# The first unit of a fused attention and feed-forward kernel on natural key and value tiles, with its band masks added by matmul

## The chip, the cores and the metric

The kernel runs on one core of a Trainium2 chip. The metric is the device time of one execution in microseconds (us); lower is better. Six executions of the kernel before took 213.77 to 217.03 us, with a median of 214.46. A profile of one execution shows, for each engine, what ran when: PE (TensorE, the matmuls) with its weight loads (PEld), DVE (VectorE), ACT (ScalarE), POOL (GpSimd) and SP (SyncE, which here only issues DMA transfers).

## The reference

Inputs are q, k and v of shape (4 batches, 8 heads, 768 positions, 64), and two weight matrices, w_in (512 x 2048) and w_out (2048 x 512), all float32. Each position attends to the positions closer than 16 and to 24 block summaries; a feed-forward layer follows.

```python
block, window = (32, 16)
k_sum = k.reshape(B, H, nb, block, D).max(axis=3)
v_sum = v.reshape(B, H, nb, block, D).mean(axis=3)
scores_l = scale * q @ k^T                       # kept where |i - j| < 16
scores_s = scale * q @ k_sum^T + log(block)      # 24 columns
a = softmax(concat(scores_l masked, scores_s))
x = a @ concat(v, v_sum)                         # (4*768) x 512
h = x @ w_in;  g = h * sigmoid(1.702 * h);  out = g @ w_out
```

## The kernel before

**Units.** The 3072 tokens are worked in eight units of 384: unit u is half u%2 of batch u//2. A unit needs the attention of its half (four pairs of heads p = 0 to 3, a pair fills the 128 partitions), gives the transposed result xT (four tiles of 128 x 384), and then 64 matmuls `ph` with w_in (`ff_in`), each four followed by a sigmoid-GELU on ACT into `gT`. For units 0 and 1, `ff_out` multiplies `gT` by w_out (`po`). For the later batches the second matrix product is done as seven products instead of eight on groups of tiles: three groups a, b, c (class `Pair`), with products p1 to p7 written a1, b1 and so on, on sums formed on DVE; their accumulators are named px, pw and py. While PE does one unit's feed-forward, the attention of the next unit is put between its matmuls.

**Order.** Every engine's instructions are kept in the order in which the program text records them (class `_Ordered`), so a waiting instruction holds up all behind it on its engine. The text of lines 817 to 957 is the order of the first unit, written out by hand; `plan0` and `plan1` (lines 961 to 964) place attention steps between the `ff_out` matmuls of units 0 and 1; `todo`, `first` and `second` place others after a given `ff_in` group `nt`; `order` and `meet` (lines 1026 to 1030) give the sequence of the seven-product matmuls and the attention steps of the next batch after each of them ("s"/"S" scores with exponential and mask of a pair, "v"/"V" the value multiply of two pairs with its normalisation, "x"/"X" the transposition of the result, small letters for the first half of the batch).

**Score tiles.** A tile of 64 queries meets 128 key columns of `kx`: its own 64 keys, 32 neighbours of either side as far as needed, and for most units the 24 block sums. `score_tiles` does 12 matmuls per pair into one two-bank tile (`psb`, two buffers), ACT takes the exponential (128 x 768, `a_sb`), DVE multiplies by the 0/1 mask `mk` (in the first unit `mk0`), and PE multiplies with the rows of `vw`, which hold the values in the same arrangement (65th column of ones for the denominator). Values lie in `vw` twice: even tiles e=0 and odd tiles e=1 (`v_odd` copies even to odd, then row copies and block-sum copies on SP's queue, `halo_odd`, `halo_even`, `sum_dmas`, overwrite the neighbour and block-sum rows).

**The first unit.** k and q come on SP's queue, are cast, and transposed by matmul (`k_turn`, `q_turn`); `k_own` copies the transposed keys into `kx`, `k_max` reduces block maxima, `k_blocks` copies them into `ksz`, `k_sides` copies the 32 neighbour columns. Values come through POOL's queue (`load_v0`, tile `vb`); `v_own`, `v_even`, `v_before`, `v_after` copy them into `vw`. The block part is apart: `b_turn`, `b_exp`, `v_sum`, `v_copy` and `av_blocks`. `s_turn`, `s_exp`, `s_mask`, `av_near`, `v_norm` and `x_turn` take a pair through attention, and `ff_first` does the first two `ph` groups as the four xT tiles appear. w_in is loaded in four pieces of 512 columns on POOL's queue (`load_w_in`), the first piece early, one in the midst, two at the end, followed by the second half of q and four pieces of w_out.

**Batch 1** is loaded during unit 0 and its values are doubled on POOL after `load_qc(1)` (line 1016); PE transposes its keys in unit 1 (`tk` at nt 2, 4, 6, 8). **Batches 2 and 3** have `v_odd(n)` on POOL at the start of unit 2b (line 1063).

Of the kernel before, what the change touches and what calls it, by code (L numbers as in the profile page):

```python
# [13 lines left out]
ALU = mybir.AluOpType  # L14
# [21 lines left out]
def kernel(  # L36
# [66 lines left out]
    def load_v0(h0, h1):  # L103
        if h0 == 0:
            early["v"] = stage.tile([128, H, NJ, D], BF16, name="vb", tag="vf")
        pool.dma_start(out=early["v"][:, h0:h1].rearrange("p h j d -> p (h j) d"),
                       in_=v[0, h0:h1].rearrange("h s d -> (h s) d")
                       .rearrange("(a p) d -> p a d", p=128))
# [23 lines left out]
    def v_odd(b):  # L132
        for p in range(NP):
            r = rows_of(b % 2, p)
            pool.tensor_copy(out=r[:, :, 1], in_=r[:, :, 0])
# [30 lines left out]
    mk0 = consts.tile([128, 2, QT], BF16, name="mk0")  # L166
    dve.memset(mk0, 1.0)

    def masks0():
        reach = window - 1  # L170
        for e, own, side in ((0, 0, 96), (1, QT, 0)):
            sel(mk0[:, e, :], reach - own, -1, 1)
            sel(mk0[:, e, :], reach + own, 1, -1)
            pool.memset(mk0[side:side + 32, e, :], 1.0)
        sel(mk0[96:128, 0, :], reach - 32, -1, 1)
        sel(mk0[0:32, 1, :], reach - QT, 1, -1)
# [51 lines left out]
    def clear0(eng):  # L228

        for p in range(NP):  # L230
            eng.memset(kx[p][0][:, 0, 96:128], 0.0)
            k4 = kx[p][0].rearrange("p (j e) c -> p j e c", e=2)
            eng.memset(k4[:, JH:NJ, 0, 88:96], 0.0)
            eng.memset(k4[:, JH:NJ, 1, 24:32], 0.0)
            eng.memset(kx[p][0][:, NQ - 1, 48:64], 0.0)
        w5 = vw[0].rearrange("p (j e) h c -> p j e h c", e=2)
        eng.memset(w5[:, :, :, :, D:VC], 1.0)
        eng.memset(w5[64:96, JH:NJ, 0, :, D:VC], float(block))
        eng.memset(w5[0:32, JH:NJ, 1, :, D:VC], float(block))
        eng.memset(vw[0][96:128, 0], 0.0)  # L240
        eng.memset(ksz, 0.0)
        eng.memset(vs4, 0.0)
        v6 = vs4.rearrange("p (a g) c -> p a g c", g=4)
        for g in range(4):
            eng.memset(v6[g * 32:g * 32 + nb, :, g, D:D + 1], float(block))

    def load_w_in(c):
        wi = moe_w_in.rearrange("(ko ki) n -> ki ko n", ki=128)
        pool.dma_start(out=w_in_sb[:, :, c * 512:(c + 1) * 512],
                       in_=wi[:, :, c * 512:(c + 1) * 512])  # L250
# [46 lines left out]
    def raw_v(p):  # L297
        return early["v"][:, 2 * p:2 * p + 2].rearrange("p h j d -> p j h d")
# [20 lines left out]

    def idle(n):  # L320

        bank = st.get("idle")
        if bank is None:
            bank = next((t for t in two if any(t is r for r in read)), None)
        if bank is None:
            return
        for i in range(n):
            pe.matmul(out=bank[:, 0:128], lhsT=warm[:, 0:128], rhs=warm[:, 0:128],
                      start=True, stop=True)


    two, read = [], []

    def opened(t):
        two.append(t)
        del two[:-2]
# [79 lines left out]

    def k_own(p, eng):

        copy(eng, at(flat_kx(p, 0), 0, [[768, 2], [256, JH], [192, 2], [1, 64]]),
             at(st["K", p], 0, [[512, 2], [128, JH], [64, 2], [1, 64]]))  # L420

    def k_max(p):
        st["m", p] = ks0[p]
        dve.tensor_reduce(out=ks0[p].rearrange("p (j e n) -> p j e n", e=2, n=2),
                          in_=at(flat_kx(p, 0), 0, [[256, NJ], [192, 2], [block, 2], [1, block]]),
                          axis=AX.X, op=ALU.max)

    def k_blocks(p, eng):

        eng.tensor_copy(out=ksz[0:64, p, 0:nb], in_=st["m", p][0:64])  # L430
        eng.tensor_copy(out=ksz[64:128, p, 32:32 + nb], in_=st["m", p][64:128])

    def k_sides(p, eng):

        flat = flat_kx(p, 0)
        eng.tensor_copy(out=at(flat, 64, [[256, JH], [96, 2], [1, 32]]),
                        in_=at(flat, 192, [[256, JH], [-160, 2], [1, 32]]))
        eng.tensor_copy(out=at(flat, 256 + 96, [[256, JH], [-224, 2], [1, 32]]),
                        in_=at(flat, 256 - 32, [[256, JH], [32, 2], [1, 32]]))
# [10 lines left out]
    def q_copy(p, eng, half=0):  # L450

        if half == 0:
            copy(eng, qT[p][0][:, 0:HALF], st["Q", p][:, 0:HALF])
            if p == NP - 1:
                st["idle"] = st["Q", p]
# [4 lines left out]
    def s_turn(p):  # L460

        big = st["S", p] = psb.tile([128, 1024], F32, name="ps_s", tag="big")
        opened(big)
        score_tiles(big, p, 0, 0)
# [9 lines left out]
    def s_exp(p):  # L474
        a = a_sb[p] = attp.tile([128, 2, TH, QT], BF16, name="a_sb", tag="a_sb")
        act.activation(out=a.rearrange("p h t c -> p h (t c)"),
                       in_=st["S", p].rearrange("p (h c) -> p h c", h=2)[:, :, 0:HALF],
                       func=ACT.Exp, scale=scale)
        read.append(st["S", p])

    def s_mask(p, eng):
        a = a_sb[p].rearrange("p h (j e) c -> p (h j) (e c)", e=2)
        eng.tensor_mul(a, a, mk0.rearrange("p e c -> p (e c)").unsqueeze(1)
                       .to_broadcast([128, 2 * JH, 2 * QT]))
# [13 lines left out]
    def v_own(p, eng):  # L498

        copy(eng, rows_of(0, p)[:, 0:JH, 1], raw_v(p)[:, 0:JH])  # L500

    def v_even(p, eng):
        copy(eng, rows_of(0, p)[0:96, 0:JH, 0], raw_v(p)[0:96, 0:JH])

    def v_before(p, eng):

        copy(eng, rows_of(0, p)[96:128, 1:JH, 0], raw_v(p)[96:128, 0:JH - 1])

    def v_after(p, eng):
        copy(eng, rows_of(0, p)[0:32, 0:JH, 1], raw_v(p)[0:32, 1:JH + 1])  # L510

    def v_sum(p):
# [4 lines left out]
        for j in range(NJ):  # L517
            o = 20 - 4 * j
            pe.matmul(out=st["VT"][r, p * 128:p * 128 + 128], lhsT=E[:, o:o + 64],
                      rhs=early["v"][:, 2 * p:2 * p + 2, j],  # L520
# [12 lines left out]
    def av_near(p):  # L533

        if p == 0:
            st["idle"] = None
        st["V", p] = pmm.tile([128, 512], F32, name="ps_av", tag="mm")
        for hh in range(2):
            for j in range(JH):
                for e in range(2):  # L540
                    t = 2 * j + e
                    pe.matmul(out=pv_of(p)[e * 64:e * 64 + 64, hh, j, 0:D + 1],
                              lhsT=a_sb[p][:, hh, t, :],
                              rhs=vw[0][:, t, 2 * p + hh, 0:D + 1],
                              start=(hh == 0 and j == 0), stop=False, skip_group_check=True)
# [15 lines left out]
    def x_turn(p):  # L561
        src = x_sb.pop(p)
        st["X", p] = psb.tile([128, 2048], F16, name="ps_x", tag="big")
        opened(st["X", p])
# [266 lines left out]
    k_turn(1)  # L831
    k_own(0, act)
    cast_k(dve, 2, 0)
    cast_k(dve, 2, 1)
    k_sides(0, pool)
    load_v0(0, 2)
# [5 lines left out]
    k_blocks(0, dve)  # L842
    cast_k(act, 3, 0)
    k_sides(1, pool)
    k_own(2, act)
    cast_k(act, 3, 1)
    k_max(1)
    cast_q(pool, 1, 0)
    cast_q(act, 0, 0)
    k_sides(2, pool)  # L850
    k_turn(3)
    k_own(3, act)
    k_blocks(1, dve)
# [3 lines left out]
    cast_q(pool, 3, 0)  # L857
    load_w_in(0)
    k_max(2)
    cast_q(dve, 2, 0)  # L860
    k_blocks(2, pool)
    q_turn(2)
    k_max(3)
    q_copy(1, act)
    s_turn(0)
    k_sides(3, dve)
    dve.tensor_copy(out=identx, in_=ident)
    q_turn(3)
    q_copy(2, act)
    s_turn(1)  # L870
    k_blocks(3, pool)
    b_turn(0)
    b_turn(2)
    s_exp(0)
    b_turn(1)
    q_copy(3, dve)
    s_mask(0, dve)
    v_own(0, pool)
    v_even(0, pool)
    v_before(0, dve)  # L880
    v_after(0, dve)
    s_exp(1)
    v_sum(0)
    s_turn(2)
    b_exp(0)
    v_copy(0, act)
    v_own(1, pool)
    v_even(1, pool)
    b_turn(3)
    s_mask(1, dve)  # L890
    v_before(1, dve)
    v_after(1, dve)
    v_sum(1)
    s_turn(3)
    s_exp(2)
    v_copy(1, act)
    av_near(0)
    av_blocks(0, 0, D + 1)
    v_own(2, pool)
    v_even(2, pool)  # L900
    s_mask(2, dve)
    b_exp(1)
    v_norm(0)
    v_before(2, dve)
    v_after(2, dve)
    v_sum(2)
    s_exp(3)
    av_near(1)
    av_blocks(1, 0, D + 1)
    v_own(3, pool)  # L910
    v_even(3, act)
    v_copy(2, dve)
    v_norm(1)
    x_turn(0)
    v_sum(3)
    v_before(3, dve)
    v_after(3, dve)
    s_mask(3, dve)
    load_w_in(1)
    copy(act, xT[0][0], st["X", 0][:, 0:HALF])  # L920
    av_near(2)
    av_blocks(2, 0, D + 1)
    v_copy(3, act)
    x_turn(1)
    v_norm(2)
# [3 lines left out]
    copy(act, xT[0][1], st["X", 1][:, 0:HALF])  # L929
# [9 lines left out]
    load_w_in(2)  # L939
    load_w_in(3)  # L940
# [4 lines left out]
    for p in range(NP):  # L945
        pool.tensor_copy(out=rows_of(0, p)[:, JH:NJ, 0], in_=raw_v(p)[:, JH:NJ])
        dve.tensor_copy(out=rows_of(0, p)[:, JH:NJ, 1], in_=raw_v(p)[:, JH:NJ])
# [44 lines left out]
    for u in range(2):  # L992
# [4 lines left out]
        else:  # L997
            todo = {2: [lambda: tk(0, 1)], 4: [lambda: tk(1, 1)], 6: [lambda: tk(2, 1)],
                    8: [lambda: tk(3, 1), lambda: load_kc(2), lambda: load_vc(2)],
                    14: [lambda: halo_odd(w51, 0), lambda: vsum(1, range(NJ))],  # L1000
# [12 lines left out]
        if u == 0:  # L1013
            beside(1, -1)
            load_qc(1)
            v_odd(1)
# [5 lines left out]
        for i, (ms, part) in enumerate(order):  # L1022
# [3 lines left out]
    order = ["a7", "a6", "a2", "a5", "b1", "a3", "b7", "a4", "b6", "b2", "b5",  # L1026
             "c1", "b3", "c7", "c6", "c2", "c5", "b4", "c3", "c4"]
    meet = {"a7": ["s0", "s1"], "b1": ["v0"], "b7": ["x0", "s2", "s3"], "b2": ["v1"],
            "c1": ["x1", "S0", "S1"], "c6": ["V0"], "c5": ["X0", "S2", "S3"], "c3": ["V1"],
# [14 lines left out]
    for b in range(1, B):  # L1044
# [17 lines left out]
        if more:  # L1062
            v_odd(n)
# [65 lines left out]
```

## Time and profile before

| | us |
|---|---|
| median of six runs | 214.46 (213.77 to 217.03) |
| the profiled execution | 215.11 |
| its span in the profile | 213.4 |
| PE busy | 200.5 (94%) |
| DVE busy | 135.9 (64%) |
| ACT busy | 124.1 (58%) |
| POOL busy | 97.9 (46%) |
| start of the dense `ph` matmuls of unit 0 | 26.11 |

Span is from the first to the last event of the profiled execution. PE's busy time includes modelled ends of pipelined matmuls. All operations are recorded through one helper, so their line is that helper's (L28), and they have to be told apart by tiles: `out<-in` names the tile written and those read. An arrow after the idle time before an instruction names what released it. Engine names with a q (SPq, POOLq) are the issuing side of DMA transfers.

### The profile page before, as it was taken

Reading aid. Unit: us, or ns where it says so; the run is one execution under the profiler, and the core shown is the slowest. Engines: PE = TensorE matmul, PEld = TensorE weight load, DVE = VectorE, ACT = ScalarE, POOL = GpSimd, SP = SyncE. Lnnn points to the kernel's source line nnn. Section 1 sums busy time; section 2 is a strip of 40 time slices with the busy share of each in tenths; the row PEclk is TensorE's granted clock in tenths of the full one; section 3 lists DMA queues with packets and bytes.
Section 4 is the critical chain, followed back from the end, with each engine's and each line's share of the span. In section 5 each row is a group of like instructions: output and inputs, shape, how many; then the busy total and the mean of one; then the engine's idle time right before and its main releaser. Section 6 shows DMA issues by size and latency. Waiting matters only on the chain.

```text
span 213.4 us, 5415 instructions
## 1 busy us (share of the span) xinstructions
PE 200.5 (94%) x2138; PEld 135.4 (63%) x2138; DVE 135.9 (64%) x377; ACT 124.1 (58%) x238; POOL 97.9 (46%) x192
## 2 busy tenths in 40 slices
PE   7767699999999899999999999999999999999994
PEld 3335465555655466656778876566788866668883
DVE  5789866562994477969978760896666820357332
ACT  2658478354667459767823477587544667772120
POOL 5799988869899999108999200000000000000000
PEclk9969999999999999999999999999999999999999
DMA  5996999999999999979999948870084150000223
GB/s 150 304 136 102 164 276 208 208 166 175 212 99 161 185 184 176 124 143 209 175 152 179 202 149 148 194 146 14 0 95 124 45 187 0 0 0 28 74 74 123
DMA packets 97832, 29.31 MB, mean 137 GB/s; under 512 B 84384, under 2 KB 95328, under 8 KB 97808
## 3 DMA queue, kind: packets, MB, share of 16 engines
q0 software_dynamic: 66960, 12.85, 72.4%
q1 hardware_dynamic: 30848, 16.13, 31.4%
q8 instruction: 16, 0.26, 0.5%
q14 instruction: 8, 0.07, 0.1%
HBM read 27.26 MB, written 6.29 MB: 157 GB/s over the span
## 4 chain that ended last, share of the span: by engine, by line
PE 61%; DMA 18%; POOL 9%; DVE 3%; ACT 3%; SPq 2%; issue 2%
PE ph L28 29%; PE px L28 14%; DMA w_out_sb<-in_moe_w_out_dram 9%; PE pw L28 7%; POOL vw L28 5%; DMA vw<-in_v_dram 3%; DMA vw<-vs 3%; PE py L28 3%; PE ps_av L28 3%; SPq L28 2%; PE po L28 2%; PE ps_s L28 2%; DMA kf<-in_k_dram 2%; DVE ks L28 2%; ACT a_sb L28 1%
## 5 line engine op out<-in xcount | busy, mean ns | idle before, releaser
L28 PE MATMUL ph<-xT,w_in_sb 128*128 128x384 f16 x512 | 85.9, 326 | 1.1 <-DVE xT L28 1.1
L28 ACT ACTIVATE gT<-ph 128x384 f16<-128x384 f32 x128 | 60.9, 490 | 27.1 <-PE ph L28 26.9
L28 PEld LDWEIGHTS <-w_in_sb 128*128 128x128 f16 x512 | 49.4, 98 | 33.1 <-issue 1.3
L28 PEld LDWEIGHTS <-gT 128*128 128x128 f16 x384 | 36.1, 98 | 12.2
L28 ACT ACTIVATE a_sb<-ps_s 128x768 bf16<-128x768 f32 x32 | 24.5, 806 | 14.4 <-PE ps_s L28 14.4
L28 POOL DMA_DIRECT2D kb<-in_k_dram x24 | 19.8, 852 | 13.7 <-DMA kx<-kb 10.7
L28 DVE TENSOR_TENSOR a_sb<-a_sb,mk 128x768 bf16<-128x768 bf16 x32 | 18.2, 571 | 10.2 <-ACT a_sb L28 8.8
L28 PE MATMUL po<-w_out_sb,gT 128*128 128x512 f16 x96 | 23.1, 380 | 0.0
L28 PEld LDWEIGHTS <-ss 128*128 128x128 f16 x216 | 20.4, 98 | 3.9 <-issue 1.3
L28 ACT ACTIVATE t<-px 128x256 f32<-128x256 f32 x21 | 8.1, 383 | 23.6 <-PE px L28 22.4
L28 POOL DMA_DIRECT2D qb<-in_q_dram x24 | 19.8, 868 | 1.4 <-DMA vw<-in_v_dram 1.3
L28 PE MATMUL px<-ta,ss 128*128 128x256 f16 x144 | 18.7, 273 | 0.9 <-ACT t L28 0.9
L28 DVE TENSOR_TENSOR ss<-gT 128x512 f16<-128x512 f16 (+3 forms) x21 | 8.0, 380 | 16.7 <-ACT gT L28 16.7
L28 PE MATMUL pw<-tb,gT 128*128 128x256 f16 x144 | 18.6, 273 | 0.0
L28 DVE TENSOR_REDUCE ks<-kx 128x24 bf16<-128x768 bf16 x12 | 11.4, 949 | 9.3 <-DMA kx<-kb 9.2
L28 DVE TENSOR_TENSOR x<-ps_av,rc 128x384 f16<-128x384 f32 x28 | 15.6, 558 | 1.0
L28 POOL DMA_DIRECT2D vw<-in_v_dram x18 | 15.9, 936 | 0.3 <-issue 0.3
L28 ACT ACT_TABLE_LOAD x10 | 12.8, 1283 | 1.0 <-PEq L1113 0.8
L28 DVE TENSOR_TENSOR osb<-pw,t 128x256 f32<-128x256 f32 x18 | 7.6, 421 | 7.1 <-ACT t L28 3.6
L28 PEld LDWEIGHTS <-a_sb 128*64 128x64 bf16 x384 | 7.9, 111 | 5.7 <-issue 2.4
L28 PE MATMUL ps_av<-vw,a_sb 128*64 128x65 bf16 x384 | 9.8, 197 | 1.4 <-DMA vw<-vs 0.8
L28 DVE RECIPROCAL rc<-ps_av 128x6 f32<-128x6 f32 x32 | 6.1, 189 | 6.9 <-PE ps_av L28 6.3
(94 smaller groups left out, 231.7 us busy)
## 6 DMA issues: line engine op xcount, KB each, us to landing
out_dram<-osb SPq DMA_DIRECT2D x18, 256.0 KB, 4.9
kb<-in_k_dram POOLq DMA_DIRECT2D x24, 96.0 KB, 6.3
vw<-in_v_dram POOLq DMA_DIRECT2D x18, 128.0 KB, 6.2
qb<-in_q_dram POOLq DMA_DIRECT2D x24, 96.0 KB, 6.4
w_in_sb<-in_moe_w_in_dram POOLq DMA_DIRECT2D x4, 512.0 KB, 7.7
w_out_sb<-in_moe_w_out_dram POOLq DMA_DIRECT2D x4, 512.0 KB, 17.0
kf<-in_k_dram SPq DMA_DIRECT2D x8, 192.0 KB, 4.1
out_dram<-osb SPq DMA_DIRECT2D x12, 128.0 KB, 1.7
```

The costliest lines, as they stand in the source:

```text
L28: r = f(*a, **kw)
```

## The change

In the first unit, keys stay in natural tiles of 128 (`own_keys`, in the second key buffer), and values are used straight from `vb`, which gets a column of ones. A pair's scores are 128 queries by 128 keys for each of three tiles, a piece of 16 queries that reach the tile before and a piece of 32 that reach the tile after, packed in 512 columns per head. A mask of 0 and -30000 (`mk0`) is written into the same accumulator first, by a matmul with the identity, so the multiplication after the exponential is gone; the exponential covers 128 x 1024. The copies `k_sides`, `v_own`, `v_even`, `v_before`, `v_after` and `s_mask` go; `k_tiles` later copies the key tiles that the second half needs. The hand-written order of the first unit is rewritten: the second query copy and three of the four `v_copy` are on DVE, one `k_blocks` on ACT, two query casts on DVE; w_in comes in pieces of 256, 256, 512, 512 and 512 columns, all issued before the second half of q. `v_odd` runs on DVE, for batch 1 at nt 13 of unit 1, for batches 2 and 3 at nt 6 of unit 2b. `order` and `meet` are changed.

```diff
     def load_v0(h0, h1):
         if h0 == 0:
-            early["v"] = stage.tile([128, H, NJ, D], BF16, name="vb", tag="vf")
+            early["v"] = stage.tile([128, H, NJ, VC], BF16, name="vb", tag="vf")
+            dve.memset(early["v"][..., D:VC], 1.0)
...
     def v_odd(b):
-            pool.tensor_copy(out=r[:, :, 1], in_=r[:, :, 0])
+            dve.tensor_copy(out=r[:, :, 1], in_=r[:, :, 0])
...
-    mk0 = consts.tile([128, 2, QT], BF16, name="mk0")
+    mk0 = consts.tile([128, 512], BF16, name="mk0")
+    BEFORE, AFTER, SIDE = HALF, HALF + 2 * window, 2 * window
     def masks0():
+        def out(ap, base, pattern, cp):
+            pool.affine_select(out=ap, in_=ap, compare_op=ALU.is_ge, fill=-30000.0,
+                               base=base, pattern=pattern, channel_multiplier=cp)
...
+    def own_keys(p):
+        return flat_kx(p, 1)[:, 0:S]
     def k_own(p, eng):
-        copy(eng, at(flat_kx(p, 0), 0, [[768, 2], [256, JH], [192, 2], [1, 64]]),
-             at(st["K", p], 0, [[512, 2], [128, JH], [64, 2], [1, 64]]))
+        copy(eng, own_keys(p).rearrange("p (e c) -> p e c", e=2),
+             at(st["K", p], 0, [[512, 2], [1, HALF]]))
...
     def s_turn(p):
-        score_tiles(big, p, 0, 0)
+        for h in range(2):
+            pe.matmul(out=big[:, h * 512:(h + 1) * 512], lhsT=ident, rhs=mk0, start=True,
+                      stop=False, skip_group_check=True)
+        def part(col, kj, q0, n):
+            for h in range(2):
+                r = slice(h * 64, h * 64 + 64)
+                pe.matmul(out=big[:, h * 512 + col:h * 512 + col + n],
+                          lhsT=own_keys(p)[r, kj * 128:(kj + 1) * 128],
+                          rhs=qT[p][0][r, q0:q0 + n], start=False, stop=True, skip_group_check=True)
+        for j in range(JH):
+            part(j * 128, j, j * 128, 128)
+            part(AFTER + j * SIDE, j + 1, j * 128 + 128 - SIDE, SIDE)
+            if j:
+                part(BEFORE + (j - 1) * window, j - 1, j * 128, window)
...
     def av_near(p):
+        def part(hh, j, q0, col, n, vj, first=False):
+            pe.matmul(out=pv_of(p)[q0:q0 + n, hh, j, 0:D + 1], lhsT=a_sb[p][:, hh, col:col + n],
+                      rhs=early["v"][:, 2 * p + hh, vj, 0:D + 1], start=first, stop=False,
+                      skip_group_check=True)
...
+    load_w_in(0, 256)
...
+    load_w_in(256, 512)
...
+    load_w_in(512, 1024)
...
+    load_w_in(1024, 1536)
+    load_w_in(1536, 2048)
...
+                    13: [lambda: v_odd(1)],
                     14: [lambda: halo_odd(w51, 0), lambda: vsum(1, range(NJ))],
...
-            v_odd(1)
             busy(6)
...
-    order = ["a7", "a6", "a2", "a5", "b1", "a3", "b7", "a4", "b6", "b2", "b5",
+    order = ["a7", "a2", "a6", "b1", "a5", "b7", "a3", "a4", "b6", "b2", "b5",
              "c1", "b3", "c7", "c6", "c2", "c5", "b4", "c3", "c4"]
-    meet = {"a7": ["s0", "s1"], "b1": ["v0"], "b7": ["x0", "s2", "s3"], "b2": ["v1"],
-            "c1": ["x1", "S0", "S1"], "c6": ["V0"], "c5": ["X0", "S2", "S3"], "c3": ["V1"],
+    meet = {"a7": ["s0", "s1"], "a5": ["v0"], "a4": ["x0", "s2", "s3"], "b5": ["v1"],
+            "b3": ["x1", "S0", "S1"], "c6": ["V0"], "c5": ["X0", "S2", "S3"], "c3": ["V1"],
             "c4": ["X1"]}
...
-            v_odd(n)
+            first.setdefault(6, []).append(lambda: v_odd(n))
```

## The prediction

> **What bounds the kernel now.** I read the busy slices of the profile's page first, then the timeline of the first 27 us, the same stretch in windows of 1 us, the chain that ended last, and the list of waits. Bare figures such as 26.11 are us from the start of the span.
>
> ```profile
> PE   7767699999999899999999999999999999999994
> ...
> PEclk9969999999999999999999999999999999999999
> ```
>
> Each digit covers 5.3 us. From the sixth on TensorE (PE) is full: the kernel is bound by its matmuls, and time is to be had in two places alone, the 26 us before that, and the few waits inside the full stretch. The timeline around 26 us shows where the dense stretch begins (columns: start, length, engine, operation, operands, count, idle time before and its releaser):
>
> ```profile
> 24.14 0.56 DVE L28 TENSOR_TENSOR x_sb<-ps_av,rc 128x384 f16<-128x384 f32 x1
> ...
> 24.61 0.35 DVE L28 COPY xT<-ps_x 128x384 f16<-128x384 f16 x1
> 25.01 0.48 PE L28 MATMUL ph<-xT,w_in_sb 128*128 128x384 f16 x2 [0.65 <-DVE xT L28]
> ...
> 25.33 0.33 PE L28 MATMUL ps_x<-identx,x_sb 128*128 128x128 f16 x3
> ...
> 25.70 0.36 DVE L28 COPY xT<-ps_x 128x384 f16<-128x384 f16 x1 [0.74 <-PE ps_x L28]
> ...
> 26.11 9.59 PE L28 MATMUL ph<-xT,w_in_sb 128*128 128x384 f16 x58 [0.45 <-DVE xT L28]
> ```
>
> The last normalised pair (x_sb, ready at 24.70) is 1.41 us ahead of the dense stretch. Windows of the start (window; busy time and count of PE, PEld, DVE, ACT, POOL; granted clock; DMA share; GB/s):
>
> ```profile
> 11.00:12.00 1.00, 0.00 (x0) 0.00 (x0) 0.95 (x3) 0.69 (x2) 1.00 (x3) 1.00 2.06 132
> 12.00:13.00 1.00, 0.33 (x3) 0.31 (x3) 1.00 (x2) 0.00 (x0) 1.00 (x4) 0.87 2.15 138
> 13.00:14.00 1.00, 1.00 (x6) 0.38 (x3) 1.00 (x3) 0.49 (x1) 1.00 (x3) 0.50 1.88 120
> ...
> 15.00:16.00 1.00, 1.00 (x17) 0.56 (x16) 0.68 (x2) 0.62 (x2) 0.84 (x4) 0.50 2.14 136
> 16.00:17.00 1.00, 1.00 (x22) 0.78 (x20) 0.94 (x3) 1.00 (x3) 1.00 (x3) 0.92 1.18 160
> ```
>
> DVE and POOL are full while PE idles, and after that idle time the granted clock is halved from 12.9 to 16.1. Two waits of the dense stretch matter, from the timeline:
>
> ```profile
> 59.00 3.25 POOL L28 COPY vw<-vw 128x768 bf16<-128x768 bf16 x4
> ...
> 61.47 2.04 DVE L28 COPY kx<-ks 128x288 bf16<-128x288 bf16 x1
> ...
> 62.28 2.66 SPq L28 DMA_DIRECT2D vw<-vw  x4
> ...
> 72.33 0.46 PEld L28 LDWEIGHTS <-a_sb 128*64 128x64 bf16 x23 [0.87 <-DMA vw<-vs]
> ...
> 106.94 1.03 PE L28 MATMUL px<-ta,ss 128*128 128x256 f16 x8 [0.48 <-ACT t L28]
> ```
>
> and from the chain:
>
> ```profile
> 65.93 6.35 DMA vw<-vs
> 72.33 0.57 PE ps_av L28 x21
> ```
>
> (In the chain: start, length, what.) The doubling of batch 1's values on POOL (59.00 to 62.25) releases four row copies and two block-sum copies on SP's queue; the last is issued at 65.93, lands 6.35 later, and PE has stood 0.87. The wait at 106.94 returns near 152 (0.9 in the list for two).
>
> **The change, part by part.**
>
> *Work removed before 26 us.* DVE: four mask products (0.69+0.53+0.53+0.53), eight value pieces (0.92+0.95+0.54+0.86), one pair of key sides (0.58): 6.1 us. POOL: three pairs of key sides (1.01+0.67+0.84) and seven value copies (4.59+0.50): 7.6. ACT: one value copy, 0.52. With them goes the order DVE mask, then value multiply: a value multiply now waits for the exponential alone.
>
> *Work added.* PE: eight mask matmuls of 512 columns. The dense `po` matmuls of that width go 8 in 1.83, so 0.23 each, 0.46 for a pair. Scores: 16 pieces, not 12; 24 of such score matmuls take 0.52, so I take 0.025 a piece, 0.40 for the 16. A head pair's scores so occupy PE 0.86 instead of 0.28 (17.74 to 18.02). Values: 6 large and 10 small pieces, some 0.63 instead of 0.31; the 16- and 32-column pieces have no row, and I price them as the 64-column ones. ACT: exponentials of 1024 columns; 0.49 for 384 and 0.81 for 768 give 1.02, so 4x0.21; two small key-sum copies (0.44, as the two `vs` copies); against that one query copy (0.49) and two pairs of `vs` copies (0.88) go to DVE. DVE: those, and a memset (0.1 to 0.28 by its value memsets).
>
> *The new start, step by step.* ACT's key copies are unchanged and end at 11.30. Block sums 0.44, first query copy 0.48: 12.2. PE has the first mask pair done by then, in its idle time. Score pieces of pair 0 to 12.6, third query turn 0.17, pair 1 to 13.6. Exponential 0 stands behind the third query copy: 13.4 to 14.4; then 1 to 15.4, block exponential 0.49, 2 to 16.9, block exponential, 3 to 18.3. PE: last query turn, two block scores, two value sums (12 matmuls, 0.67) to 14.7; scores 2 to 15.5; two block scores; scores 3 to 16.9; values 0 and 1 (0.63+0.28 each) to 18.7; value sums to 19.3; a transpose 0.17; values 2 to 20.4; transpose, first `ph` pair (0.35), values 3 to 21.8. Normalising from 22.0 to 22.75, then the same 1.41: dense at 24.2, 1.9 us before 26.11. I take 1.5, because the small pieces and 0.05 at each hand-over are only approximate. Upper bound: if the PE additions hide under ACT's row of exponentials, 2.6. Lower bound: clock halved again (below), 0.2.
>
> *The clock.* From 9.4 to 12.9 PE was busy some 1.3 us (0.87 between 10 and 11, none, then 0.3); in the new order it works about 2.2 in that stretch (the mask pair and scores 0, the third turn and half a mask pair are added). I take full speed, since the gaps are smaller. If it falls anyway, everything between 12.9 and 16.1 lasts twice as long: scores 2 end at 17.2, scores 3 at 18.5, the dense stretch starts at 25.9. [...]
>
> *w_in in five pieces.* POOL issues five loads at 0.75 instead of four: +0.75, against 7.6 removed. Its order is now the three value loads (from 6.5, not 7.96), a query cast, then w_in pieces between the key-sum copies, so it is past w_in near 17.3 instead of 22.3, and the queries and four w_out loads follow 4 us earlier. DMA stands nearly still from 19 to 22 now (share 0.15); that hole goes. The first piece is needed at 20.5; before, the value loads had drained by about 17, so I expect 18 to 19.5. w_out last landed at 45.14 with its matmuls at 47.21; both move earlier, w_out more. Cost nothing, covered by 1 us at the first piece; if that cover is gone, the first `ph` pair waits by the excess. Value loads starting at 8.5 run into the queries' (until 10.7); a query cast late by 1 us on DVE and POOL still precedes its PE use (13.7).
>
> *Rest of unit 0.* DVE copies both value parities for the second half (8 copies for 4, +2 us), POOL four key tiles. Row copies leave SP at about 28, as now; their reader runs at 41.65 less the shift, and last landed before 38.3. Nothing.
>
> *Value doubling on DVE, batch 1.* It is now behind DVE's fourth key turn. Those steps take 1.8 us each when POOL is quiet (57.39 to 59.15) and start at 53.50 less the shift; with 0.8 of disturbance from POOL's load issues, as at 54.84, they end near 61.5 less the shift, instead of 63.5 now. Four copies of 768: between 0.35 (288 columns take 0.22, 144 take 0.19) and 0.81 (POOL's own); I take 0.38, nearest the DVE rows, so 1.5. Ready at 63.0 less the shift. SP then needs four issues of 0.62 and one of 0.84, 3.45 to its last issue (3.65 now), and 6.35 to 7 to land, because POOL's next key loads, no longer behind the copies, now start 6 us earlier and fill the queues. PE restarts at 73.1 less the shift, against 72.33: of 1.5, 0.7 is left, and the wait grows from 0.87 to some 1.7. Bounds for this one term: 0.8 less (no disturbance) to 1.7 more (rival 2). What queues behind the copies on DVE: the `vs` casts (1.12), still done before SP reaches the block sums.
>
> [...]
>
> *Doubling, batches 2 and 3.* DVE idles 2.0 before 92.54 and 7.2 before 134.20; 1.5 fits, and SP's row copies start only at 96.80 and 138.12. Nothing.
>
> *Order of the last products.* `a5` now has `b1` between it and `a6`: t2 is copied at 106.90, `a5` would come at 107.1, so 0.48 and 0.45 go. Late next: the scores before `V0` now lead it by two products, 2.31 us, not three; the masks are ready 2.5 to 2.7 after the scores, so some 0.15 returns, twice. Net 0.65.
>
> **Sum.** 1.5 - 0.8 + 0.65 = 1.35 us. The profiled execution took 215.11 (span 213.4 and 1.7 around it), 0.65 over the median of the runs shown; I subtract from the median 214.46: 213.1.
>
> **Rivals.**
> 1. The clock halves again: 0.2 at the start, which becomes 0.6 lost at 72 us (73.1 - 0.2 against 72.33), and 0.65 from the order: about 214.4. For it: the start still has PE gaps near 9 and 11.5. Against: busier than before.
> 2. Slower: the doubling becomes the bound at 72 us. If POOL's issues slow the fourth key turn by another 0.8 and each copy costs POOL's 0.81, it is ready at 65.5 less 1.5, so 64.0; PE restarts 10.1 later, at 74.1, 1.8 after now; less 0.65 that is +1.1, 215.6. It decides from readiness at 62.9 (there the 0.65 is used up). For: the 2.04 row. Against: POOL then issues loads and does not copy; under such issues the product rows keep 0.67.
> 3. The first w_in piece or value loads land late: each us over 20.5 costs one at the start, up to 1.5; ends near 214.5.
>
> **How the numbers follow.** This measurement can tell about 0.3% (0.64 us). Forecast 0.53 (own range 212.2 to 213.8), rivals 1 and 3 together 0.25, rival 2 0.22. The forecast gives faster 0.50, same 0.03; 1 and 3 give 0.08, 0.13 and slower 0.04; 2 gives same 0.04, slower 0.18. So 0.58, 0.20, 0.22. The range: a start of 2.6 with half the disturbance of DVE (2.6 - 0.4 + 0.65) gives 211.6; rival 2 gives 215.6.
>
> **What would show it.** Dense `ph` begins at 24.2 to 24.8; no mask product of 128x768 before it; granted clock 1.00 from 12 to 16; w_in landing before 20.5; doubling on DVE done by 61.5 and the wait for vw<-vs near 1.7; no wait of px for t at 105 and 150. Wrong if the clock is halved there, if that wait passes 3, or if PE pieces in the first 22 us leave no gap at all and end later.

## The result, and the profile after

The change makes the kernel slower by 0.6%: the ratio of the changed kernel's time to the time before is 1.0061, with an interval of 1.0038 to 1.0083. The medians are 217.27 us (38 executions, 213.83 to 219.04) and 214.65 us. The ratio leaves out executions over 1.5% above the fastest of their kernel, 23 of the 39 that are listed singly for the changed kernel, so the medians stand further apart than the ratio. By their mean granted clock these 39 fall into three groups: 4 at 1.00 took 213.83 to 215.47, 17 at 0.99 took 214.74 to 217.39, and 18 at 0.98 took 217.23 to 219.04. One stretch of 3.41 us at half clock, as it is met below, lowers the mean over 214.7 us by 0.008, so by estimate these are executions with none, about one and about two such stretches. The profiled one has one; where the second stands no profile of this kernel shows. The profiled execution took 216.38 with a span of 214.7, against 215.11 and 213.4 before.

The busy slices of the page, after:

```profile
PEclk9999999999999889999999999999999999999999
```

Before, the lowered clock stood in the third slice; now it stands in the fourteenth and fifteenth, at 70 to 80 us. The start itself did what was forecast (timeline of the changed kernel, around 23 us):

```profile
23.18 0.48 PE L28 MATMUL ph<-xT,w_in_sb 128*128 128x384 f16 x2 [0.65 <-DVE xT L28]
...
24.28 9.59 PE L28 MATMUL ph<-xT,w_in_sb 128*128 128x384 f16 x58 [0.45 <-DVE xT L28]
```

The dense stretch begins at 24.28 instead of 26.11, so PE comes to 70 us 1.83 ahead. There it loses all of that and more. The same timeline around the first values of unit 2:

```profile
56.76 6.61 POOL L28 DMA_DIRECT2D kb<-in_k_dram  x8 [2.24 <-PE ps_t L28]
...
59.53 1.79 DVE L28 COPY vw<-vw 128x768 bf16<-128x768 bf16 x4
...
61.40 2.68 SPq L28 DMA_DIRECT2D vw<-vw  x4
63.34 5.28 POOL L28 DMA_DIRECT2D vw<-in_v_dram  x6
64.19 1.91 SPq L28 DMA_DIRECT2D vw<-vs  x2
...
71.33 0.19 PE L28 MATMUL ps_av<-vw,a_sb 128*64 128x65 bf16 x1 [1.82 <-DMA vw<-vs]
73.17 0.60 PE L28 MATMUL ps_av<-vw,a_sb 128*64 128x65 bf16 x23 [1.65 <-DMA vw<-vs]
...
74.46 3.13 PE L28 MATMUL po<-w_out_sb,gT 128*128 128x512 f16 x8
```

The doubling on DVE is done at 61.3, earlier than POOL's 62.25 before. SP issues the last block-sum copy at 65.13, not 65.93. Yet PE, which is through with its earlier work at 69.51, waits twice, until 73.17, 3.65 in all with one matmul of 0.19 in it. The list of waits and the chain agree on what ends it:

```profile
PE ps_av L28 <- DMA vw<-vs: 3.5, 2, 1.8
```

```profile
65.13 7.99 DMA vw<-vs
```

The copy takes 7.99 from its issue to its landing; before it took 6.35. The last line of the timeline above shows the second loss: eight `po` matmuls take 3.13, elsewhere 1.90. Windows of 3.41 us there (window; busy time and count of PE, PEld, DVE, ACT, POOL; granted clock; DMA share; GB/s):

```profile
66.74:70.15 3.41, 2.77 (x22) 1.45 (x20) 1.07 (x2) 1.22 (x2) 3.08 (x5) 1.00 2.47 168
70.15:73.56 3.41, 0.58 (x24) 0.50 (x24) 0.00 (x0) 0.00 (x0) 2.09 (x3) 1.00 2.03 181
73.56:76.97 3.41, 3.41 (x41) 1.62 (x35) 2.53 (x6) 2.05 (x3) 3.06 (x4) 0.50 2.40 154
```

Here a window in which PE worked for 0.58 us was followed by one at a granted clock of 0.50.

**The sum, by marks on PE** (after minus before, profiled executions):

| mark | before | after | lag | what happened in between |
|---|---|---|---|---|
| dense `ph` of unit 0 | 26.11 | 24.28 | -1.83 | the new start |
| second values matmul of unit 2 | 72.33 | 73.17 | +0.84 | the wait for the sum copies, 2.67 lost |
| second `ph` stretch of unit 2 | 82.83 | 85.23 | +2.40 | the half clock, 1.56 lost |
| `ph` of batch 2's last unit | 125.95 | 127.78 | +1.83 | the new order, 0.57 won |
| `ph` of batch 3's last unit | 171.00 | 172.27 | +1.27 | the new order again, 0.56 won |

The last lag is that of the spans, 214.7 and 213.4.

### The profile page after: what moved, and what is told of

It reads as the page before. It is cut to its first block, busy times and chain, and to the rows that moved or that the text cites. A ratio compares the mean times of both kernels' runs of the same rounds, so it can differ in the third digit from the quotient of the medians.

```text
span 214.7 us, 5472 instructions
## 1 busy us (share of the span) xinstructions
PE 202.9 (95%) x2178; PEld 137.1 (64%) x2178; DVE 130.1 (61%) x377; ACT 123.6 (58%) x234; POOL 82.8 (39%) x165
## 4 chain that ended last, share of the span: by engine, by line
PE 82%; DVE 6%; DMA 6%; SPq 2%; ACT 2%; issue 1%
PE ph L28 35%; PE px L28 15%; PE pw L28 8%; PE po L28 8%; PE ps_av L28 5%; PE ps_s L28 4%; PE py L28 4%; DMA vw<-vs 4%; SPq L28 2%; DVE kx L28 2%; DMA kf<-in_k_dram 2%; DVE ks L28 2%; ACT kx L28 1%; PE ps_x L28 1%; DVE qT L28 1%
## 5 line engine op out<-in xcount | busy, mean ns | idle before, releaser
L28 ACT ACTIVATE a_sb<-ps_s 128x768 bf16<-128x768 f32 x28 | 21.2, 806 | 15.9 <-PE ps_s L28 15.9
L28 PE MATMUL po<-w_out_sb,gT 128*128 128x512 f16 x96 | 24.3, 395 | 0.0
L28 PEld LDWEIGHTS <-ss 128*128 128x128 f16 x216 | 20.9, 98 | 2.6
L28 DVE TENSOR_TENSOR a_sb<-a_sb,mk 128x768 bf16<-128x768 bf16 x28 | 15.6, 558 | 10.3 <-ACT a_sb L28 8.5
L28 PE MATMUL ps_av<-vw,a_sb 128*64 128x65 bf16 x336 | 8.2, 198 | 3.5 <-DMA vw<-vs 3.5
L28 PEld LDWEIGHTS <-a_sb 128*64 128x64 bf16 x336 | 6.6, 111 | 7.3 <-issue 4.3
```

What stands on the lines that cost most here:

```text
L28: r = f(*a, **kw)
```

## Experiments

Two theories stood for the wait. **Theory 1**: the doubling left POOL, so POOL goes on at once with its loads of batch 2's keys and values, 7.2 us earlier (56.76, before 63.97); the theory takes it that these share the DMA engines with the sum copies, which land late. **Theory 2**: doubling on DVE behind its last key turn makes the issue late for a PE that now arrives earlier, whatever the loads do. Every ratio below is to the kernel before.

**1. Hold all of POOL's loads until the sum copies have landed.** In the changed kernel:

```
-                    8: [lambda: tk(3, 1), lambda: load_kc(2), lambda: load_vc(2)],
+                    8: [lambda: tk(3, 1)],
...
-                         lambda: sum_dmas(w51, 0)]}
+                         lambda: sum_dmas(w51, 0), lambda: hold(),
+                         lambda: load_kc(2), lambda: load_vc(2)]}
...
+    def hold():
+        pool.tensor_copy(out=held_at[0:32, 0], in_=w51[64:96, NJ - 1, 0, 0, 0:8])
+        pool.tensor_copy(out=held_at[0:32, 1], in_=w51[0:32, NJ - 1, 1, 0, 0:8])
```

> The changed kernel with POOL's loads of batch 2's keys and values held until both block-sum copies have landed: two small copies on POOL read the rows that these write. Theory 1 (shared DMA engines): the sum copies, last issued at 65.1 still, land within 3.5 to 4.5 us, at 68.5 to 69.5; PE waits under 0.3, the clock stays full, and the span is 209.6 to 210.6. Theory 2 (the issue is too late whatever else moves): they land 6 us or more after the last issue, at 71 or later, the wait is 1.5 or more and the span 212 to 214.7. Neither expects a wait for the later loads: the key turns of batch 2 come after 90.

Its timeline:

```profile
64.32 1.75 SPq L28 DMA_DIRECT2D vw<-vs  x2
...
68.54 0.18 POOL L28 COPY held_at<-vw 32x8 bf16<-32x8 bf16 x1 [0.62 <-DMA vw<-vs]
69.06 6.57 POOL L28 DMA_DIRECT2D kb<-in_k_dram  x8 [0.33 <-issue]
...
70.06 0.57 PE L28 MATMUL ps_av<-vw,a_sb 128*64 128x65 bf16 x24
...
91.58 9.59 PE L28 MATMUL ph<-xT,w_in_sb 128*128 128x384 f16 x58 [0.86 <-DMA xT<-x]
109.64 0.22 PE L28 MATMUL ps_av<-vw,a_sb 128*64 128x65 bf16 x1 [2.66 <-DVE a_sb L28]
110.75 0.57 PE L28 MATMUL ps_av<-vw,a_sb 128*64 128x65 bf16 x23 [0.89 <-DMA vw<-vs]
```

The last copy, issued at 65.3, has landed at 68.5: 3.3 us, not 7.99, and PE goes through at 70.06 without a wait. So the landing follows theory 1. The time does not: 218.87, a ratio of 1.0179 (1.0111 to 1.0246), a span of 216.5 where I expected 210. The loads, 12 us later, now stand beside the transfers of batch 2, and PE waits 0.86, 2.66 and 0.89 there, with half clock from 111.36 to 114.77 behind it. That "neither expects a wait for the later loads" was wrong. The loads' own data do not come late: the keys are issued by 75.6 and take at most 7.8 to land, and what reads them is issued from 85.55. Late are the copies that SP issues beside POOL's loads: the transposing copy `xT<-x` takes 8.24 from 83.30, a sum copy 7.50 from 103.20, and the wait of 2.66 is for DVE, which in this execution stood 13.0 in all for the transposing copies of the keys (6.2 in the change).

**2. Hold only the values.** The same `hold`, with `load_kc(2)` left in its place.

> The changed kernel with POOL's loads of batch 2's keys where they are (57 to 63.5) and only its loads of the values held until the block-sum copies have landed: half of the dose. Theory 1 (shared DMA engines): landing 5 to 6.5 us after the last issue at 65.1, between the 3.3 with all loads held and the 8.0 with none; PE waits 0.6 to 2 us and the clock stays full; span 210.5 to 212.2. Theory 2 (the issue alone is late): 8.0 again, 214.7.

The last copy was issued at 66.61 and landed 4.67 later; the waits of its timeline are short at 71 us, but not those in batch 2:

```profile
70.87 0.19 PE L28 MATMUL ps_av<-vw,a_sb 128*64 128x65 bf16 x1 [0.54 <-DMA vw<-vs]
71.33 0.57 PE L28 MATMUL ps_av<-vw,a_sb 128*64 128x65 bf16 x23 [0.26 <-DMA vw<-vs]
...
108.45 0.19 PE L28 MATMUL ps_av<-vw,a_sb 128*64 128x65 bf16 x1 [1.24 <-DVE osb L28]
109.86 0.57 PE L28 MATMUL ps_av<-vw,a_sb 128*64 128x65 bf16 x23 [1.22 <-DMA vw<-vs]
```

Time 217.88, ratio 1.0126 (1.0063 to 1.0190), span 215.7. The landing again goes by the loads, and is even shorter than the 5 to 6.5 expected; the gain is again given back one batch later, with half clock from 111.12 to 114.53 behind the waits.

**3. Loads where the kernel before has them.** The doubling stays on DVE; one small POOL copy reads the block sums that DVE has cast, so the loads, moved behind it as in the first experiment, begin just after that.

```
+    def hold():
+        pool.tensor_copy(out=held_at[0:32], in_=vs[0:32, :, 0:8])
```

> The changed kernel with POOL's loads of batch 2's keys and values held only until DVE has cast the block sums (a small copy on POOL reads them), so that they start near 62.7, about as long ahead of the last block-sum copy (65.1) as in the kernel before, where they start at 63.97 and it at 65.93. The doubling stays on DVE. Theory 1 (shared DMA engines; the copies land the later, the longer the loads have run): 6.2 to 6.8 us to land, at 71.4 to 71.9, which is what the prediction had; PE waits 1.6 to 2.2 instead of 3.65; span 211.4 to 211.9 if the clock stays full and 1.5 more if it is halved behind the wait. Later batches lose nothing, since the loads stand where the kernel before has them. Theory 2 (the late issue alone): landing after 8.0, a wait of 3.65, span 214.7.

Its timeline:

```profile
62.57 0.23 POOL L28 COPY held_at<-vs 32x64 bf16<-32x64 bf16 x1 [6.18 <-DVE vs L28]
63.06 6.57 POOL L28 DMA_DIRECT2D kb<-in_k_dram  x8 [0.26 <-issue]
...
69.91 0.57 PE L28 MATMUL ps_av<-vw,a_sb 128*64 128x65 bf16 x24
```

No wait there: issued at 64.6, landed by 69.91, so within 5.3. One for the same kind of copy is left in batch 2:

```profile
106.84 0.57 PE L28 MATMUL ps_av<-vw,a_sb 128*64 128x65 bf16 x23 [0.90 <-DMA vw<-vs]
```

Time 212.91, ratio 0.9941 (0.9911 to 0.9972), span 211.0, clock 1.00. Theory 2 has fallen: with the doubling on DVE as in the change, the start and the order as in the change, and nothing else moved than POOL's loads by 6.3 us, the loss becomes a gain. I had expected a wait of 1.6 to 2.2 at 70 us, and there is none; I had also said that later batches lose nothing, and from the `ph` of batch 2 (89.42) to that of its last unit (124.08) it is 34.66, 1.1 more than in the change. Of the earlier landing, 0.5 is the issue, 64.6 instead of 65.13, and the rows of the four DVE copies say why (minimum, median and maximum of one in ns, then first and last start); the change first, then this kernel:

```profile
L28 DVE COPY vw<-vw x4: 341/496/698, 59.5 to 61.0; 128x768 bf16<-128x768 bf16 x4
```

```profile
L28 DVE COPY vw<-vw x4: 350/352/353, 59.6 to 60.4; 128x768 bf16<-128x768 bf16 x4
```

While POOL issued loads (56.76 to 63.37 in the change), a copy of 0.35 took up to 0.70.

**4. Doubling on POOL again, ahead of its loads.** Batches 2 and 3 keep it on DVE.

```
-                    13: [lambda: v_odd(1)],
...
             load_qc(1)
+            v_odd(1, pool)
             busy(6)
```

> The changed kernel with batch 1's value doubling on POOL again, ahead of POOL's loads of batch 2's keys (DVE keeps the doubling of batches 2 and 3). Both theories: the four copies run on POOL between 54 and 58, so SP issues the block-sum copies behind DVE's casts of the sums, the last at 63 to 63.5 instead of 65.1. Theory 1 (the copies land late because POOL's loads of batch 2 share the DMA engines): they still take 7 to 8 us to land, at 70.5 to 71.5; PE, there at 69.5, waits 1 to 2 us; clock not halved; span 211.3 to 212.3 against 214.7. Theory 2 (the doubling on DVE makes the issue late, and that alone is the loss): they take 6.35 as before, land at 69.7, the wait is under 0.3 and the span 210.2 to 210.7.

Its timeline:

```profile
52.94 3.17 POOL L28 COPY vw<-vw 128x768 bf16<-128x768 bf16 x4
...
57.83 6.57 POOL L28 DMA_DIRECT2D kb<-in_k_dram  x8
...
70.94 0.56 PE L28 MATMUL ps_av<-vw,a_sb 128*64 128x65 bf16 x23 [0.34 <-DMA vw<-vs]
```

The last sum copy goes out at 64.01 and lands 6.89 later; a wait of 0.34 is left. Time 212.39, ratio 0.9874 (0.9808 to 0.9940), span 210.9. Neither theory was met: the landing lies between the two figures, and issue and landing gave some 1.1 each. The same kernel again, for a narrower interval:

> The same kernel as in the first experiment (the change, with batch 1's doubling back on POOL ahead of its key loads), run again for a narrower interval: 212.4 against 214.5, a ratio of 0.990 with an interval that ends below 0.994.

It gave 212.12 us and a ratio of 0.9892 (0.9862 to 0.9922), with no wait for `vw<-vs` among PE's; a version 1.1% faster than the kernel before.

**5. Keep PE at work during the wait.** Twelve dummy matmuls ahead of the waiting values of unit 2 (the trace holds records of eleven):

```
             elif what[0] == "v":
+                if u == 2 and i == 0:
+                    warmth(12)
```

> The changed kernel with twelve dummy matmuls of 512 columns on PE just ahead of the first values of unit 2; their results are read by nobody, the outputs are unchanged. They take 2.5 to 3 us of the 3.65 that PE stands there. Theory 1 and 2 both leave the landing of the sum copies at 73.1. If the half clock from 73.56 to 76.98 follows from PE's idle time, it is gone, the eight po matmuls behind the values take 1.9 instead of 3.13, and the span falls by 1.5 to 213.1 to 213.3. If the half clock has another cause, the span stays at 214.7 or grows.

Its timeline:

```profile
72.25 2.54 PE L28 MATMUL ps_w<-warm 128*128 128x512 bf16 x11
...
75.42 0.56 PE L28 MATMUL ps_av<-vw,a_sb 128*64 128x65 bf16 x23 [0.49 <-DMA vw<-vs]
...
76.38 1.90 PE L28 MATMUL po<-w_out_sb,gT 128*128 128x512 f16 x8
```

The copies landed late as before (8.18 after issue), but the eight `po` take 1.90, and from the second values matmul to unit 2's first `ph` stretch it is 7.57 (75.42 to 82.99), against 9.13 in the change (73.17 to 82.30). With PE at work through the wait the granted clock stayed at 1.00 (windows 73.74 to 77.15 and 77.15 to 80.56), so the half clock of the change came with PE's idle time and cost 1.56. The time is 214.95, ratio 1.0014 (0.9924 to 1.0104). The profiled execution's span, 215.4, is not below 214.7, because its clock was halved in the start instead (0.50 from 8.89 to past 15), where the dense stretch began at 26.97; the other three took 214.01 to 215.23 at full clock.

**6. The order of the last products, undone and alone.** In the changed kernel with the old `order` and `meet`:

> The changed kernel with the order of the last products and the pieces they meet as before the change. The waits of px for t at about 107 and 152 return with 0.45 each, and up to 0.55 each if the accounting of the two traces is right: span 0.9 to 1.1 above 214.7, 215.6 to 215.8. If the new order gives nothing, 214.7.

and the kernel before with the new ones:

> The kernel before with nothing changed but the order of the last products and what they meet. The prediction had 0.65 for it, the accounting of the two traces 1.14, the experiment with the old order in the changed kernel 0.99: span 212.3 to 212.8 against 213.4, no wait of px for t at 107 and 152.

The first took 220.06, ratio 1.0204 (1.0097 to 1.0312), more than I said, since its sum copy took 9.56 to land (its issue alone took 2.54, in the change 0.97) and PE stood 5.1 us at 72. By the marks behind that, from the `ph` of one batch to those of the next, the order itself can be read alone:

| kernel | batch 2 | batch 3 |
|---|---|---|
| before | 91.83 to 125.95: 34.12 | 136.89 to 171.00: 34.11 |
| change with the old order | 95.91 to 130.02: 34.11 | 140.97 to 175.08: 34.11 |
| change | 94.24 to 127.78: 33.54 | 138.72 to 172.27: 33.55 |
| before with the new order | 90.80 to 124.34: 33.54 | 135.28 to 168.83: 33.55 |

It is worth 0.57 and 0.56, in both surroundings. The second kernel's ratio, 0.9946 (0.9902 to 0.9989), is about that; its profiled execution also had no wait at 72 us. Since the change doubles batches 2 and 3 on DVE and the kernel before on POOL, equal rows also show that this part costs nothing.

**7. The doubling of batch 1 alone.** The kernel before with `v_odd(1)` on DVE:

```
+                    13: [lambda: v_odd(1, dve)],
...
             load_qc(1)
-            v_odd(1)
```

> The kernel before with nothing changed but batch 1's doubling on DVE, behind its last key turn; POOL's loads of batch 2 then start near 61 instead of 63.97. Both theories expect a loss. The turns end at 62 to 63.5, the copies at 64 to 65, the last block-sum copy is issued at 67.5 to 69. Theory 1 (shared DMA engines): it takes 8 us or more to land, at 75.5 to 77, PE waits 4 to 5.5, the clock is halved behind that for some 3.4 us, and the span is 217.5 to 220. Theory 2 (the late issue alone): 6.35 to land, 74 to 75.3, a wait of 2.5 to 4, span 215 to 217.

In its timeline:

```profile
58.95 6.63 POOL L28 DMA_DIRECT2D kb<-in_k_dram  x8
```

and in its chain:

```profile
66.28 7.87 DMA vw<-vs
```

A ratio of 1.0116 (1.0038 to 1.0194), 218.86 (four executions, 215.85 to 222.30; the profiled one took 219.53). The copies on DVE were ready early (by 62.5, not 64 to 65), the loads began at 58.95 and not 61, and the landing of 7.87 made waits of 0.76 and 2.30, less than the 4 to 5.5 expected, with half clock from 75.71 to 79.12 behind them. So the doubling alone makes the kernel slower, by its way through the loads.

**The landing times together** (profiled executions; issue is that of the last sum copy):

| kernel | key loads from | values' loads from | issue | key loads run for | landing after issue |
|---|---|---|---|---|---|
| all loads held (1) | 69.06 | 75.56 | 65.3 | none | 3.3 |
| loads late (3) | 63.06 | 69.55 | 64.6 | 1.5 | within 5.3 |
| before | 63.97 | 70.45 | 65.93 | 2.0 | 6.35 |
| before with the new order (6) | 62.91 | 69.39 | 64.9 | 2.0 | within 6.4 |
| doubling on POOL (4) | 57.83 | 64.33 | 64.01 | 6.2 | 6.89 |
| the same again (4) | 57.81 | 64.32 | 64.0 | 6.2 | within 6.4 |
| doubling alone (7) | 58.95 | 65.53 | 66.28 | 7.3 | 7.87 |
| PE kept at work (5) | 59.44 | 66.05 | 67.20 | 7.8 | 8.18 |
| change | 56.76 | 63.34 | 65.13 | 8.4 | 7.99 |
| old order (6) | 56.95 | 63.66 | 65.43 | 8.5 | 9.56 |
| values held (2) | 57.58 | 71.87 | 66.61 | 9.0 | 4.67 |

"Within" means that PE went through without a wait, which gives an upper bound alone. The landing is shortest with no loads in flight. It is 7.87 or more in the four kernels in which POOL had begun to issue the values' loads before the copy was issued, and at most 6.89 in the others, so in these runs it goes with these loads rather than with the time that the key loads have run. The two executions of (4) differ by 0.5 or more, so smaller steps are not to be read. How much is due to which loads is known only roughly: the keys alone add 1.4 (4.67 less 3.3) and the values 3.3 (7.99 less 4.67), but in experiment 2 the copy was issued 1.5 later, 9.0 into the key loads and not 8.4. Shown is that the copies landed after 3.3 with no loads in flight and after 4.67 to 9.56 with loads in flight; that the DMA engines are what they share was not tested apart.

## Why the prediction was wrong

- **The start** was right. The step "dense at 24.2" was measured at 24.28; of it I took 1.5, and 1.83 came. It came by the path that was laid out: the last normalised pair was ready at 22.87, where 22.75 was said, and the same 1.41 followed. The granted clock was 1.00 from 12 to 16, and no mask product is left. The rival in which the clock halves again came true in one execution: the profiled one with PE kept at work had a granted clock of 0.50 there and began its dense stretch at 26.97.
- **w_in in five pieces** cost nothing, as stated: PE has no wait for it.
- **Value doubling, batch 1, is the step that failed**, in two places. Its first half held: ready at 63.0 less the shift, which with 1.83 is 61.2, and 61.3 was measured; with the stated 3.45 to the last issue that is 64.6, and it was 65.13. The copies took 0.45 each in the mean, not 0.38. Then the mis-sized term: "6.35 to 7 to land, because POOL's next key loads ... now start 6 us earlier and fill the queues". That loads in flight delay the landing is what the runs show (3.3 with all of them held); that they fill the queues was not shown, and the size was 7.99. The wait became 3.65 with one matmul within it, not 1.7. The values' loads, which follow the keys' and so were now issued ahead of the copy (63.34 against 65.13; before the change 70.45 against 65.93), are not in the prediction.
- **Missing altogether** was what such a wait does to the clock. I had weighed the clock in the start alone, and priced a wait at 72 us as its own length. The half clock behind it costs 1.56 more. Together these turn a step of 0.8 lost into 4.23 lost (2.67 and 1.56). The other two steps, 1.83 and 1.13 won, leave 1.27 lost.
- **The slower rival** had the right place and, by luck, nearly the size (1.1 lost, where the spans lose 1.27), but another mechanism: a doubling ready at 64.0. It was ready at 61.3, and the time was lost all the same, in the landing of the copies and the half clock. The sign "wrong if that wait passes 3" came true with 3.65.
- **Order of the last products**: 0.65 said, 1.13 measured. The 0.15 that was to return twice did not, and each of the two waits gave some 0.1 more than its own 0.48 or 0.45.
- **Doubling of batches 2 and 3**: nothing, as said.
- **DVE beside POOL's issues** lost less than beside POOL's copies, where a copy of 0.22 took 2.04 (61.47, before). Under POOL's issues the DVE copies grew from 0.35 to at most 0.70, while POOL's key load issues, of 0.82 each, stayed at 6.61 for eight (6.57 in experiment 3, without these copies beside them). The four copies took 1.79 instead of 1.16 (the four at 92.41, while POOL waits), so that is 0.6 us of the loss, not the bulk of it.

## What to carry to other kernels

When work is taken off an engine that also issues loads, the loads behind it move forward too (here by 7.2 us, to 56.76): find their new time and ask which short transfer that someone waits for is then in flight. Here that cost more than the start had won, and putting the loads back where they were (212.91, with 1.1 lost again in batch 2) kept most of the gain, and the work back on the issuing engine ahead of them (212.12) kept it whole. But a load has two sides: pushed past the critical copies altogether, it ran into the next batch's (218.87). And price a PE wait of some 2 us with a half clock behind it: in the change that was 1.56 us more, and five of the profiled executions have one behind waits in the dense stretch (below).

## What the runs showed of the hardware

**Half clock.** These windows of 3.41 us stand ahead of a half-clock stretch, or just ahead of such a window, with PE's busy time in them and the granted clock of the 3.41 us behind them:

| execution | window | its clock | PE busy | clock of the window behind |
|---|---|---|---|---|
| old order (6) | 71.35 to 74.76 | 1.00 | 0.19 | 0.50 |
| change | 70.15 to 73.56 | 1.00 | 0.58 | 0.50 |
| all loads held (1) | 107.95 to 111.36 | 1.00 | 0.83 | 0.50 |
| before | 9.33 to 12.74 | 1.00 | 1.00 | 0.50 |
| values held (2) | 107.71 to 111.12 | 1.00 | 1.45 | 0.50 |
| doubling alone (7) | 72.30 to 75.71 | 1.00 | 1.51 | 0.50 |
| PE kept at work (5), in its start | 5.48 to 8.89 | 1.00 | 1.73 | 0.50 |
| old order (6) | 67.94 to 71.35 | 1.00 | 1.76 | 1.00 |
| doubling alone (7) | 68.89 to 72.30 | 1.00 | 2.25 | 1.00 |
| all loads held (1) | 104.53 to 107.95 | 1.00 | 2.44 | 1.00 |
| change | 66.74 to 70.15 | 1.00 | 2.77 | 1.00 |

Two more windows had no half clock behind them: in the kernel before, PE was busy for 2.65 from 70.77 to 74.18, with its wait of 0.76 for the sum copies inside, and with PE kept at work for 2.92 from 73.74 to 77.15. The end of the changed kernel stands against the first seven: from 210.10 to 213.51 PE is busy for 1.47, and the 1.19 behind it, up to the end of the span, are at 1.00. The ends of matmuls are modelled, so 1.73 and 1.76 can't be told apart. The rows that stand close:

```profile
5.48:8.89 3.41, 1.73 (x13) 0.89 (x10) 2.28 (x4) 1.88 (x3) 3.38 (x3) 1.00 0.97 283
8.89:12.30 3.41, 2.53 (x12) 1.99 (x13) 2.49 (x5) 2.12 (x5) 0.00 (x0) 0.50 1.72 210
```

```profile
67.94:71.35 3.41, 1.76 (x13) 0.80 (x11) 0.56 (x1) 0.55 (x1) 2.63 (x4) 1.00 3.07 159
71.35:74.76 3.41, 0.19 (x1) 0.11 (x1) 0.00 (x0) 0.00 (x0) 2.04 (x3) 1.00 1.92 199
74.76:78.17 3.41, 3.14 (x51) 1.98 (x52) 2.22 (x6) 1.51 (x2) 2.69 (x4) 0.50 2.27 147
```

The single waits in the windows ahead of half clock were short: in the kernel before, the longest gap of PE from 9.33 to 12.74 is 1.80; with the values held the two waits are 1.24 and 1.22, with the doubling alone the wait is 2.30, in the change 1.65 and the end of one of 1.82. The clock was 0.50 throughout 12.74 to 16.15 before, 73.56 to 76.97 in the change, 74.76 to 78.17 with the old order, 111.36 to 114.77 with all loads held, 111.12 to 114.53 with the values held and 75.71 to 79.12 with the doubling alone; PE was busy for 3.14 (old order) or all of these 3.41 us. Behind those of the change and of the kernel before it was 1.00 again (76.97 to 80.38, 16.15 to 19.56). In the start of the execution with PE kept at work, PE was busy for 2.53 of the first 3.41 us at half clock (8.89 to 12.30), and the clock was still 0.50 in each window of 1 us up to 15.00. Why the clock falls and rises as it does, these runs do not show.
